# Pooled keys and values of two batches transposed by DMA through DRAM instead of by TensorE

## The chip, the cores and the metric

The kernel runs on one core of a Trainium2 chip. A core has a matrix engine (TensorE, PE in the profile; its weight loads are listed as PEld), a vector engine (VectorE, DVE), a scalar engine for activation functions (ScalarE, ACT), a general engine (GpSimd, POOL), and a sync engine (SyncE, SP) that here only issues DMA transfers. Each runs its own list of instructions in order and waits on semaphores for the others. PE writes its results to PSUM, here seen as eight banks of 128 partitions by 512 f32; everything else lives in SBUF or DRAM.

The metric is the device time of one execution in microseconds. For the kernel before it is 948.33 us, the median of 3 runs (948.24 to 948.73).

## The reference

Attention with a spatially reduced key side, then a two-layer network on every token:

```python
# q: (4, 12288, 128), kv: (4, 384, 32, 128), w_sr: (128, 128), all f32
kv_pool = kv.reshape(B, H // 4, 4, W // 4, 4, C).mean(axis=(2, 4))   # (4, 96, 8, 128)
k = v = kv_pool.reshape(B, 768, C) @ w_sr                            # keys are the values
a = softmax(q @ k.transpose(0, 2, 1) / sqrt(C))
x = (a @ v).reshape(49152, 128)
h = x @ w_in                                                         # (128, 2048)
out = (h * sigmoid(1.702 * h)) @ w_out                               # (2048, 128)
```

## The kernel before

**Tiling.** The 49152 tokens are cut into 96 groups of 512. For attention, group i has six chunks, one for each 128 of the 768 keys of its batch; for the network (called MoE in the code), group g has 16 chunks, one for each 128 of the 2048 hidden units. A chunk is *filled* by PE (one matmul of 512 columns into a PSUM bank: `fill_attn` L350, `fill_moe` L596), put through exp or GELU by ACT into a slot of the SBUF buffer `ag` (L352, L598), three chunks to an ACT instruction, and later *drained* by PE: `drain_attn` (L363) multiplies it with the values of its batch, `drain_moe` (L606) with a block of w_out. Fills use banks 0 to 2 and 3 to 5 in turn; drains accumulate in banks 6 and 7. DVE ends an attention tile by dividing by the sum of weights (L386, L389), and an MoE group by a transpose of 32x32 blocks from PSUM into one of three `o_sb` tiles (L617), which SP writes to DRAM with four DMAs (L619).

**Two rounds.** The attention of batches 0 and 1, then the MoE of their 48 groups, then the same for batches 2 and 3. Between, parts of x of 24 tiles are put away in DRAM by SP and brought back transposed (`put_away` L503, `bring_back` L509). During the first round's MoE these come one at a time: put away when group 9, 11, 13, 15, 17 begins, brought back when group 10, 12, 14, 16, 18 begins.

**Keys and values of batches 2 and 3** are made in the first round's MoE as well. Eight times two DMAs of POOL load and add kv over the window into an f32 tile (`add_kv`, from group 2 on for batch 2 and from group 24 on for batch 3; `gate` holds POOL back until DVE is so far). Then, for each half batch `a`, when group 12 or 14 (34 or 36) begins, `use_kv` lets DVE add the last two rows (`sum_kv`, L179: 96 pooled rows by 4 by 128 channels, bf16) and enters three steps in a list of extras: `transpose_pooled` (four PE transposes L184, a DVE copy into pT, L186), `make_k` (one matmul of 384 columns L192, a DVE copy into kT, L193) and `make_v` (three matmuls of 128 columns L199, a DVE copy into v, L201).

**What sets the order.** Each engine's order is written out by hand: a planner in the kernel's Python runs once when the program is built, with a clock `now` for PE, `end[p]` for the end of each ACT instruction and `dve` for DVE. Its unit is one matmul of 512 columns. It places fill after fill and, between them, drains and extras, while they fit ahead of the time at which the next fill is due (`limit`, L802). The times that it reckons with stand in a few constants; the lines that matter here are

```python
FIXED, CHUNK, SWITCH, HANDOVER, EVACUATE = 0.295, 1.978, 6.0, 1.0, 4.5      # L746
now = max(now, end[p - 2] + HANDOVER / 2)                                   # L786: the bank is free
begin = max(now + HANDOVER / 2, end[p - 1] if p else 0.0)                   # L788: ACT begins
limit = end[-1] - len(seq[n + 3][1]) - HANDOVER if n + 3 < len(seq) else 1e9  # L802
```

A sequence of work that DVE also helps with (exp and GELU of a few chunks by polynomials, `early_fill`, L415 and L409) is fixed in number and is placed by the same planner. `background_moe(g)` (L556) is called when the first fill of group g is placed, and enters the DMAs and extras of that group.

Of the kernel before, what the change touches and what calls it, by code (L numbers as in the profile page):

```python
# [10 lines left out]
BF = mybir.dt.bfloat16  # L11
# [13 lines left out]
def kernel(  # L25
    ctx, tc, q, kv, w_sr, moe_w_in, moe_w_out, out,
):
    nc = tc.nc
    B, N, C = q.shape
    _, H, W, _ = kv.shape  # L30
    r = 4
# [17 lines left out]
    q_flat = q.rearrange("b n c -> (b n) c")  # L49
    x_bf = nc.dram_tensor("x_bf", (B * N, C), BF, kind="Internal").ap()  # L50
    q_bf = nc.dram_tensor("q_bf", (B * N, C), BF, kind="Internal").ap()

    kv_r = kv.rearrange("b (ch p) (a w) c -> b a ch p (w c)", p=128, a=2)

# [43 lines left out]
    def acc_bf():  # L98
        return acc().bitcast(BF)
# [20 lines left out]
    def new_keys(b):  # L120
        kTs[b] = kvres.tile([128, J], BF, name="kT")

        vs[b] = kvres.tile([128, JC, C + 8], BF, name="v")
        nc.vector.memset(vs[b][:, :, C:C + 1], 1.0)

    def load_chunk(b, jc):
# [51 lines left out]
        pooled[b, a] = kvtmp.tile([Hp, 4, C], BF, name="pooled")  # L178
        nc.vector.tensor_tensor(pooled[b, a], t[:, 0], t[:, 1], ADD)  # L179

    def transpose_pooled(b, a):
        ps = acc_bf()[:, 0:h].rearrange("p (a b) -> p a b", a=4)
        for wp in range(4):
            nc.tensor.transpose(ps[:, wp, :], pooled[b, a][:, wp, :], ident[:Hp, :Hp])  # L184
        pTs[b, a] = kvtmp.tile([128, h], BF, name="pT")
        nc.vector.tensor_copy(pTs[b, a], ps.rearrange("p a b -> p (a b)"))  # L186

    def make_k(b, a):
        ps = acc()
        if a == 0:  # L190
            new_keys(b)
        nc.tensor.matmul(ps[:, :h], w_sr_sb, pTs[b, a], start=True, stop=True)  # L192
        nc.vector.tensor_copy(kTs[b][:, a * h:(a + 1) * h], ps[:, :h])  # L193

    def make_v(b, a):
        ps = acc()
        pT = pTs.pop((b, a))
        for k in range(K):
            nc.tensor.matmul(ps[:, k * C:(k + 1) * C], pT[:, k * 128:(k + 1) * 128], w_sr_sb,  # L199
                             start=True, stop=True)  # L200
        nc.vector.tensor_copy(vs[b][:, a * K:(a + 1) * K, 0:C], ps[:, :h].rearrange("p (k c) -> p k c", k=K))  # L201
        for jc in range(a * K, a * K + K):
            vs[b, jc] = True

# [351 lines left out]
    def background_moe(g):  # L556

        n, g = divmod(g, 4 * XS)
        m, odd = divmod(g - 9, 2)
        m += FIRST  # L560
        if n == 0 and FIRST <= m < RT // PART:
            (bring_back if odd else put_away)(n, m)
        g += n * 4 * XS
        nonlocal low
        if g == 12:
            low = EARLY * JC
            order[:] = [f for f in order if f >= low // K]
        if g in CAST_MOE:
            gate()
            cast_q(CAST_MOE[g])  # L570
        if g in (41, 42):
            load_qT(g - 28)
        if g == 43:
            background(early[0])
        for b, lo in ((2, 2), (3, 24)):
            if lo <= g < lo + 8:
                gate()
                add_kv(b, g - lo)
            if g in (lo + 10, lo + 12):
                use_kv(b, (g - lo - 10) // 2)  # L580

    def use_kv(b, a):
        nonlocal extra_at
        sum_kv(b, a)
        on_dve(3.5)
        extra_at = max(extra_at, dve + 1.5)
        extras.extend([(transpose_pooled, b, a), (make_k, b, a), (make_v, b, a)])

    extras = []

# [120 lines left out]
    def prepare(p):  # L711
# [3 lines left out]
        for i, jc in part:  # L715
# [27 lines left out]

    FIXED, CHUNK, SWITCH, HANDOVER, EVACUATE = 0.295, 1.978, 6.0, 1.0, 4.5  # L746
    COST = {pool_chunk: (1.9, 2.6), key_chunk: (0.3, 2.4), value_chunk: (0.3, 2.4),
            transpose_q: (1.05, 4.2), early_fill: (1.0, 5.5), key_and_value: (0.55, 3.5),
            transpose_pooled: (0.9, 3.6), make_k: (0.8, 3.2), make_v: (0.8, 3.7)}
    COPY = {pool_chunk: 1.5, key_chunk: 1.5, value_chunk: 1.5, key_and_value: 2.8, transpose_q: 3.2}  # L750
    SMALL = 0.26
    RECIPROCAL = 8.2
# [5 lines left out]
    def on_dve(cost):  # L758
        nonlocal dve
        dve = max(dve, now + 1.0) + cost  # L760
# [8 lines left out]
    def fill(p):  # L769
        nonlocal now  # L770
        if p >= len(seq):
            return
        kind, part = seq[p]
        prepare(p)
        if p == 4:
            turns.insert(0, 2)
        if p == narrow - 5:
            for m in (2, 5):
                turns.remove(m)
        if p == narrow:  # L780
            assert not any(m in closes for m in (2, 5))
            now = max(now, free.pop(2), free.pop(5))
        lo = K * (p % 2)
        (fill_attn if kind == "a" else fill_moe)(part, banks[:, lo:lo + len(part), :])
        if p >= 2:
            now = max(now, end[p - 2] + HANDOVER / 2)  # L786
        now += len(part)
        begin = max(now + HANDOVER / 2, end[p - 1] if p else 0.0)  # L788
        if p and kind != seq[p - 1][0]:
            begin += SWITCH  # L790
        end.append(begin + FIXED + CHUNK * len(part))
# [5 lines left out]
    for n in range(len(seq)):  # L797
        fill(n + 2)
        jobs(n + 3)
        while True:  # L800
            room = room_ahead()
            limit = end[-1] - len(seq[n + 3][1]) - HANDOVER if n + 3 < len(seq) else 1e9  # L802
            bank = free[next_acc()]
            f = None
            if extras and now >= max(extra_at, bank):
                f, *args = extras[0]
            if steps and dve <= now + 2.0:
                early_step()
            near = todo and todo[0][0] == "m" and todo[0][2] > 10
            if not f and not near and not steps and early_todo and early_fits(min(n + 2, len(seq) - 1), *early_todo[0]) and dve <= now + 2.0 and now >= bank:  # L810
                f, args = early_fill, early_todo[0]
            if f and max(now, bank) + COST[f][0] > limit + (0.0 if f is early_fill else 4.5) and room >= 4 * K:
                f = None
            if f:
                now = max(now, bank) + COST[f][0]
                f(*args)
                free[last_acc] = dve + 1.0 if f is early_fill else copied(f)
                if f in (transpose_pooled, make_k, make_v):
                    on_dve(2.5)
                extra_at = max(now + PAUSE, dve + 1.5 if f in (transpose_pooled, make_k, make_v) else 0.0)  # L820
                if f is early_fill:
                    pass
                else:
                    extras.pop(0)
                continue
            if not source:

                if todo_early and not any(early_waits(t) for t in range(todo_early[0][1], todo_early[0][1] + TS)):
                    source = todo_early
                else:  # L830
                    source = todo
            if not source:
                break
            kind, i, c = source[0]
            needs = at[("at" if kind == "a" else kind, i, c)]
            cost = K * SMALL if kind == "a" else 1.0
            halved = kind == "a" and i // TS < SPLIT
            first_of = (c == 0 or halved) and (kind == "m" or i % TS == 0)
            if source is not todo_early and (needs > n or (kind == "a" and first_of and at["at", i + TS - 1, c if halved else 1] > n)
                                             or (kind == "m" and first_of and (i, FCH - 1) in lent  # L840
                                                 and made.get((i, FCH - 1), 1e9) > now + 1.0)
                                             or (kind == "a" and (early_waits(i) or first_of and early_waits(i + TS - 1)))):
                if first_of:
                    source = None
                break
            start = now if source is todo_early else max(now, end[needs] + HANDOVER)
            if first_of:
                start = max(start, bank)
            if start + cost > limit and not (room < 2 * K + 1 or (room < 4 * K and start == now)):
                if first_of:  # L850
                    source = None
                break
            now = start + cost
            (drain_attn if kind == "a" else drain_moe)(i, c)
            source.pop(0)
            if kind == "a" and i // 4 in early:
                early_left -= 1
                if not early_left:
                    low = 0
            if (halved or c == (1 if kind == "a" else FCH - 1)) and (kind == "m" or i % TS == TS - 1):  # L860
                source = None
# [31 lines left out]
```

## Time and profile before

| | |
|---|---|
| median of 3 runs | 948.33 us (948.24 to 948.73) |
| span of the profiled execution, first to last instruction | 946.7 us |
| PE busy | 933.9 us (99%) |
| ACT busy | 933.5 us (99%) |
| DVE busy | 575.1 us (61%) |
| granted TensorE clock | 1.00 throughout |
| DMA, mean over the span | 101 GB/s |
| L184, 16 transposes of pooled keys, mean of one record | 205 ns |
| L199, 12 value matmuls, mean of one record | 219 ns |

The profile is one execution recorded by the hardware. A group in it is named by line, engine and operation, with the tile written and the tiles read (out<-in); the mean is the length of one record. Records of PE overlap, since a matmul begins before the one before it has left the array, so that the time that a matmul costs is read from the chain of waits, where each piece begins as the last one ends. SPq and POOLq are the queues of DMA issues; the time to landing of a DMA runs from its issue to its completion. "Idle before <- X" names what ended a wait.

### The profile page before, as it was taken

What the parts mean: (1) busy time and instruction counts of PE and PEld (TensorE: products, weight loads), DVE (VectorE), ACT (ScalarE), POOL (GpSimd) and SP (SyncE); (2) the same over time, 40 slices, a digit from 0 to 9 for tenths busy, and PEclk for the clock granted to TensorE, in tenths of its full rate; (3) what the DMA queues carried; (4) which work ended last, traced back from release to release, by engine and by line L of the source; (5) the groups of instructions that cost most, each with busy time, mean ns of one, the idle gap of its engine ahead of it and who ended that gap; (6) DMA issues with size and microseconds to landing.
All of it is one profiled execution on the core that took longest, in us unless ns stands there. A gap on an engine that the chain in (4) does not pass through costs nothing.

```text
span 946.7 us, 15374 instructions
## 1 busy us (share of the span) xinstructions
PE 933.9 (99%) x6200; PEld 502.5 (53%) x6314; DVE 575.1 (61%) x1091; ACT 933.5 (99%) x709; POOL 66.5 (7%) x115
## 2 busy tenths in 40 slices
PE   8999999999999999999999999999999999999998
PEld 4677776444444444444446777744444444444444
DVE  5753653011678776667765765376767766777651
ACT  6999999999999999999999999999999999999998
POOL 3101001330000232000000000000000000000000
PEclk9999999999999999999999999999999999999999
DMA  9997943999867799865335683552222222222222
GB/s 210 195 207 168 181 92 52 130 163 170 164 117 114 119 147 119 127 99 87 56 58 105 138 170 84 119 123 42 36 39 40 38 41 34 44 34 45 34 45 46
DMA packets 372856, 95.46 MB, mean 101 GB/s; under 512 B 346720, under 2 KB 370400, under 8 KB 372320
## 3 DMA queue, kind: packets, MB, share of 16 engines
q1 hardware_dynamic: 344000, 62.36, 36.9%
q0 software_dynamic: 28512, 31.99, 22.3%
q8 instruction: 49, 0.80, 0.3%
q14 instruction: 23, 0.19, 0.1%
q10 hardware_dynamic: 272, 0.13, 0.0%
HBM read 52.49 MB, written 48.76 MB: 107 GB/s over the span
## 4 chain that ended last, share of the span: by engine, by line
PE 97%; ACT 1%; DMA 1%; issue 1%; DVE 0%; POOL 0%; POOLq 0%
PE banks L606 35%; PE banks L596 34%; PE banks L363 14%; PE banks L350 12%; ACT ag L352 1%; PE banks L415 1%; DMA x<-in_kv_dram 1%; PE banks L139 0%; PE banks L409 0%; PE banks L634 0%; PE banks L236 0%; POOL x L222 0%; PE banks L161 0%; PE banks L294 0%; PE banks L192 0%
## 5 line engine op out<-in xcount | busy, mean ns | idle before, releaser
L598 ACT ACTIVATE ag<-banks 128x1536 bf16<-128x1536 f32 (+1 forms) x509 | 681.1, 1489 | 0.0
L596 PE MATMUL banks<-x,w_in_sb 128*128 128x512 bf16 x1476 | 405.8, 379 | 1.7
L606 PE MATMUL banks<-ag,w_out_sb 128*128 128x512 bf16 x1477 | 402.6, 379 | 1.7
L352 ACT ACTIVATE ag<-banks 128x1536 bf16<-128x1536 f32 (+2 forms) x192 | 245.6, 1421 | 3.5 <-PE banks L236 2.3
L606 PEld LDWEIGHTS <-w_out_sb 128*128 128x128 bf16 x1520 | 148.3, 98 | 177.2 <-issue 0.2
L596 PEld LDWEIGHTS <-w_in_sb 128*128 128x128 bf16 x1519 | 147.1, 98 | 171.3 <-issue 0.7
L617 DVE STREAM_TRANSPOSE o_sb<-banks 128x512 f32<-128x512 f32 x95 | 68.1, 717 | 171.4 <-PE banks L606 166.9
L363 PEld LDWEIGHTS <-ag 128*128 128x128 bf16 x2268 | 145.5, 98 | 44.6 <-issue 0.3
L363 PE MATMUL banks<-v,ag 128*128 128x129 bf16 x2268 | 163.0, 220 | 0.2
L350 PE MATMUL banks<-qT,kT 128*128 128x512 bf16 x498 | 145.0, 379 | 3.5 <-ACT ag L352 0.5
L442 DVE SCALAR_TENSOR_TENSOR ea<-ea,eb 128x512 f32<-128x512 f32 x132 | 90.4, 685 | 3.7 <-DVE ea L442 0.7
L386 DVE RECIPROCAL rec<-banks 128x3 f32<-128x3 f32 x124 | 22.3, 180 | 85.3 <-PE banks L363 84.9
L389 DVE TENSOR_TENSOR x<-banks,rec 128x384 bf16<-128x384 f32 x124 | 69.1, 557 | 4.3
L350 PEld LDWEIGHTS <-kT 128*128 128x128 bf16 x543 | 45.8, 98 | 25.9 <-issue 2.0
L473 DVE RECIPROCAL eb<-ea 128x256 f32<-128x256 f32 x34 | 57.6, 1724 | 0.5
L466 DVE SCALAR_TENSOR_TENSOR ea<-ea,eb 128x512 f32<-128x512 f32 x68 | 46.5, 683 | 1.9
L173 POOL DMA_DIRECT2D kvs<-in_kv_dram x32 | 40.4, 1323 | 19.3 <-DMA kvs<-in_kv_dram 17.1
L431 DVE TENSOR_SCALAR ea<-banks 128x512 f32<-128x512 f32 x33 | 22.8, 692 | 29.6 <-PE banks L415 29.2
L521 POOL MEMSET gate_tile<- 1x1 f32 x38 | 3.4, 89 | 325.8 <-DVE gate_tile L520 325.8
L453 DVE TENSOR_SCALAR qT<-banks 128x512 f32<-128x512 f32 x17 | 11.8, 692 | 20.7 <-PE banks L409 20.6
L437 DVE SCALAR_TENSOR_TENSOR eb<-eb,ea 128x512 f32<-128x512 f32 x33 | 22.8, 691 | 0.9
L444 DVE SCALAR_TENSOR_TENSOR ag<-ea,ee 128x512 bf16<-128x512 f32 x24 | 16.6, 691 | 1.2
(83 smaller groups left out, 286.3 us busy)
## 6 DMA issues: line engine op xcount, KB each, us to landing
out_dram<-o_sb SPq DMA_DIRECT2D x380, 64.0 KB, 2.0
kvs<-in_kv_dram POOLq DMA_DIRECT2D x32, 384.0 KB, 6.3
q_bf<-in_q_dram POOLq DMA_DIRECT2D x21, 512.0 KB, 6.6
x_bf<-x SPq DMA_DIRECT2D x13, 768.0 KB, 5.6
x<-in_kv_dram POOLq DMA_DIRECT2D x11, 512.0 KB, 10.4
x_bf<-x SPq DMA_DIRECT2D x6, 384.0 KB, 4.6
x<-in_q_dram POOLq DMA_DIRECT2D x5, 256.0 KB, 15.3
x<-in_kv_dram SPq DMA_DIRECT2D x1, 1024.0 KB, 5.0
```

Source lines behind the costliest of these rows:

```text
L173: nc.gpsimd.dma_start(out=kv_sums[b][:, i2], in_=kv_p[b, i, w, :, i2], **({"accum_op": ADD} if n else {}))
L350: nc.tensor.matmul(ps[:, k, :], kTs[i // GB][:, jc * 128:(jc + 1) * 128], rhs, start=True, stop=True)
L352: nc.scalar.activation(place([("a",) + c for c in chunks]), ps, AF.Exp, scale=scale)
L363: nc.tensor.matmul(av_of[u][:, k * (C + 1):(k + 1) * (C + 1)], weights(("a", i, jc))[:, o:o + T], vs[i // GB][:, jc, 0:C + 1], start=(jc = ...
L389: nc.vector.tensor_tensor(to, ps[:, :, 0:C], rec.unsqueeze(2).broadcast_to([128, TS, C]), MUL)
L442: nc.vector.scalar_tensor_tensor(a, a, COEFFS[k], b, ADD, MUL)
L466: nc.vector.scalar_tensor_tensor(a, a, COEFFS[k], b, ADD, MUL)
L473: nc.vector.reciprocal(b[:, m:m + 256], a[:, m:m + 256])
L596: nc.tensor.matmul(ps[:, k, :], w_in_sb[:, fc * 128:(fc + 1) * 128], x[:, g % (4 * XS) * G:(g % (4 * XS) + 1) * G], start=True, stop=True)
L598: nc.scalar.activation(place([("m",) + c for c in chunks]), ps, AF.Gelu_apprx_sigmoid)
L606: nc.tensor.matmul(o_of[g], w_out_sb[:, fc, :], weights(("m", g, fc)), start=(fc == 0), stop=(fc == FCH - 1))
L617: nc.vector.transpose(o_sb, o_of.pop(g))
```

## The change

The pooled half of batches 2 and 3 is no longer transposed by PE. When group 11 (14 for the second half; 33 and 36 for batch 3) begins, DVE adds the rows as before and SP writes the pooled half to a DRAM tensor (`put_pooled`). When the next group begins, SP reads it back with a transposing DMA into pT (`turn_pooled`), and when the one after that begins, `make_k` is entered in the extras. Its kT half is written to another DRAM tensor (`put_k`) at the next step, and one group later read back by three transposing DMAs into the value tile (`turn_k`): the values are the keys transposed, so `make_v` falls away. Rows of the value tile are 144 wide instead of 136.

The planner's constants change as well: ACT's fixed part of an instruction is 0.24 instead of 0.295, and HANDOVER is split into RELEASE (0.3, end of ACT to the next fill of its banks, formerly 0.5), LATENCY (0.95, end of a fill to the start of ACT, formerly 0.5) and MARGIN (1.2 in `limit`, formerly 1.0). This moves fills and drains against each other in the whole program.

```diff
@@ -49,6 +49,8 @@
+    pool_bf = nc.dram_tensor("pool_bf", (B, 2, r, Hp, C), BF, kind="Internal").ap()
+    k_bf = nc.dram_tensor("k_bf", (B, JC, C, 128), BF, kind="Internal").ap()
...
-        vs[b] = kvres.tile([128, JC, C + 8], BF, name="v")
+        vs[b] = kvres.tile([128, JC, C + 16], BF, name="v")
...
-    def transpose_pooled(b, a):
-        ps = acc_bf()[:, 0:h].rearrange("p (a b) -> p a b", a=4)
-        for wp in range(4):
-            nc.tensor.transpose(ps[:, wp, :], pooled[b, a][:, wp, :], ident[:Hp, :Hp])
-        pTs[b, a] = kvtmp.tile([128, h], BF, name="pT")
-        nc.vector.tensor_copy(pTs[b, a], ps.rearrange("p a b -> p (a b)"))
+    def put_pooled(b, a):
+        nc.sync.dma_start(out=pool_bf[b, a].rearrange("w h c -> h w c"), in_=pooled[b, a])
+
+    def turn_pooled(b, a):
+        pTs[b, a] = kvtmp.tile([128, 1, h], BF, name="pT")
+        nc.sync.dma_start_transpose(out=pTs[b, a], in_=pool_bf[b, a].rearrange("w h c -> (w h) c"))
+
+    def put_k(b, a):
+        jc = slice(a * K, a * K + K)
+        nc.sync.dma_start(out=k_bf[b, jc].rearrange("j c t -> c j t"),
+                          in_=kTs[b][:, a * h:(a + 1) * h].rearrange("c (j t) -> c j t", t=128))
+
+    def turn_k(b, a):
+        for jc in range(a * K, a * K + K):
+            nc.sync.dma_start_transpose(out=vs[b][:, jc:jc + 1, 0:C], in_=k_bf[b, jc])
 
     def make_k(b, a):
         ps = acc()
         if a == 0:
             new_keys(b)
-        nc.tensor.matmul(ps[:, :h], w_sr_sb, pTs[b, a], start=True, stop=True)
+        nc.tensor.matmul(ps[:, :h], w_sr_sb, pTs.pop((b, a))[:, 0, :], start=True, stop=True)
         nc.vector.tensor_copy(kTs[b][:, a * h:(a + 1) * h], ps[:, :h])
-
-    def make_v(b, a):
-        ps = acc()
-        pT = pTs.pop((b, a))
-        for k in range(K):
-            nc.tensor.matmul(ps[:, k * C:(k + 1) * C], pT[:, k * 128:(k + 1) * 128], w_sr_sb,
-                             start=True, stop=True)
-        nc.vector.tensor_copy(vs[b][:, a * K:(a + 1) * K, 0:C], ps[:, :h].rearrange("p (k c) -> p k c", k=K))
...
-            if g in (lo + 10, lo + 12):
-                use_kv(b, (g - lo - 10) // 2)
-
-    def use_kv(b, a):
-        nonlocal extra_at
-        sum_kv(b, a)
-        on_dve(3.5)
-        extra_at = max(extra_at, dve + 1.5)
-        extras.extend([(transpose_pooled, b, a), (make_k, b, a), (make_v, b, a)])
+            a, step = divmod(g - lo - 9, 3)
+            if 0 <= a < 2 and step == 0:
+                sum_kv(b, a)
+                on_dve(3.5)
+                put_pooled(b, a)
+            if 0 <= a < 2 and step == 1:
+                turn_pooled(b, a)
+            if 0 <= a < 2 and step == 2:
+                extras.append((make_k, b, a))
+            if 1 <= a < 3 and step == 0:
+                put_k(b, a - 1)
+            if 1 <= a < 3 and step == 1:
+                turn_k(b, a - 1)
...
-    FIXED, CHUNK, SWITCH, HANDOVER, EVACUATE = 0.295, 1.978, 6.0, 1.0, 4.5
+    FIXED, CHUNK, SWITCH, HANDOVER, EVACUATE = 0.24, 1.978, 6.0, 1.0, 4.5
+    RELEASE, LATENCY, MARGIN = 0.3, 0.95, 1.2
     COST = {pool_chunk: (1.9, 2.6), key_chunk: (0.3, 2.4), value_chunk: (0.3, 2.4),
             transpose_q: (1.05, 4.2), early_fill: (1.0, 5.5), key_and_value: (0.55, 3.5),
-            transpose_pooled: (0.9, 3.6), make_k: (0.8, 3.2), make_v: (0.8, 3.7)}
+            make_k: (0.8, 3.2)}
...
         if p >= 2:
-            now = max(now, end[p - 2] + HANDOVER / 2)
+            now = max(now, end[p - 2] + RELEASE)
         now += len(part)
-        begin = max(now + HANDOVER / 2, end[p - 1] if p else 0.0)
+        begin = max(now + LATENCY, end[p - 1] if p else 0.0)
...
-            limit = end[-1] - len(seq[n + 3][1]) - HANDOVER if n + 3 < len(seq) else 1e9
+            limit = end[-1] - len(seq[n + 3][1]) - MARGIN if n + 3 < len(seq) else 1e9
...
-                if f in (transpose_pooled, make_k, make_v):
+                if f is make_k:
                     on_dve(2.5)
-                extra_at = max(now + PAUSE, dve + 1.5 if f in (transpose_pooled, make_k, make_v) else 0.0)
+                extra_at = max(now + PAUSE, dve + 1.5 if f is make_k else 0.0)
```

## The prediction

> **What bounds the kernel now.** I read the page's busy shares first, then the same by stages, then the chain that ended last, and last the queues that the change touches. The page:
>
> ```profile
> PE 933.9 (99%) x6200; PEld 502.5 (53%) x6314; DVE 575.1 (61%) x1091; ACT 933.5 (99%) x709; POOL 66.5 (7%) x115
> ...
> PE 97%; ACT 1%; DMA 1%; issue 1%; DVE 0%; POOL 0%; POOLq 0%
> ```
>
> and of the stages the one from 75 to 945 us (its length, then busy time and count of PE, PEld, DVE, ACT, POOL, then the granted clock, DMA share and GB/s):
>
> ```profile
> 75.00:945.00 870.00, 863.08 (x5408) 455.56 (x5506) 529.99 (x951) 867.24 (x649) 51.44 (x79) 1.00 0.56 92
> ```
>
> PE and ACT are equally busy, so the busy shares do not say which of them rules. The chain does: 97% of it is PE. In the stretch from 75 to 945 us PE's records cover 863 of 870 us, and what is missing is mostly lost records: the chain has its pieces there back to back. Around the first of the steps that go:
>
> ```profile
> 228.58 0.65 PE banks L606 x3
> 229.23 0.17 PE banks L184 x4
> 229.40 0.65 PE banks L596 x3
> 230.05 0.43 PE banks L606 x2
> 230.48 0.16 PE banks L192
> 230.64 0.65 PE banks L596 x3
> 231.29 0.43 PE banks L606 x2
> 231.72 0.17 PE banks L199 x3
> ```
>
> Each piece starts where the last one ends; a full matmul (512 columns) takes 0.216 us (0.65 for three). ACT's 501 triple instructions are 1.345 us apart (673.6 us over 501 in the groups), because PE feeds them no faster. So after the start a microsecond of PE work taken away is a microsecond won, and a microsecond that PE waits is a microsecond lost. SP's queue, and PE's supply from it, is where a wait can come from:
>
> ```profile
> 212.31 6.04 SPq L619 DMA_DIRECT2D out_dram<-o_sb  x4
> 219.87 3.29 SPq L509 DMA_TRANSPOSE x<-x_bf  x1
> 223.28 2.19 SPq L619 DMA_DIRECT2D out_dram<-o_sb  x4
> 225.57 0.45 SPq L503 DMA_DIRECT2D x_bf<-x  x1
> 226.12 4.78 SPq L619 DMA_DIRECT2D out_dram<-o_sb  x4
> 231.00 3.39 SPq L509 DMA_TRANSPOSE x<-x_bf  x1
> ```
>
> SP issues in order. Here, at the pooled keys of batch 2, it is not idle: four output writes take 2.19 us to issue, but 4.78 behind a 768 KB put-away, and a bring-back holds SP 3.4 us.
>
> **The change, part by part.** *What goes.* Per half batch PE loses four transposes (0.17 us of the chain) and three value matmuls (0.17); the key matmul (0.16) stays. Four halves: 4 x 0.34 = **1.36 us off the path**, all won. DVE loses two copies per half (L186 0.36, L201 0.56 us); DVE is idle 5.97 us ahead of each output transpose of that stretch, so that wins nothing.
>
> The Trainium skill ("TensorE: Matmul & The Clock Gate", Part 4: PE-mode transpose) gives a transpose some 275 ns in a kernel. By that the 16 would cost 4.4 us and the change would win 5.1; the chain's 0.17 us for four says 42 ns each, since they overlap in the pipeline, and I go by the chain.
>
> *What is added: PE's wait for pT.* make_k now reads a pT that comes over SP: put the pooled half into DRAM, read it back transposed, one group of 512 tokens (6.7 us) apart. PE's order is fixed, and what is queued behind make_k is everything: fills, drains, and through them ACT. So its landing time counts in full. Distances are counted in the new program's order of instructions.
>
> First half of batch 2. SP's order is: put-away, pooled put, four writes of group 8, four of group 9, bring-back, then the transposing read. Group 9's writes need its last drain matmul. PE reaches make_k 33 full matmuls after that one: 34 x 0.2157 = 7.33 us from its start. The chain to pT from the same moment: 0.4 (a matmul's record is 0.38) + 0.72 (DVE's output transpose) + 2.19 (four writes) + 0.1 (gaps) + 3.39 (bring-back) = 6.8, plus the landing of a read of 384 rows. For that the rows (the last number is the median time to landing, us) are:
>
> ```profile
> out_dram<-o_sb SPq DMA_DIRECT2D x380, 64.0 KB, 2.0
> ...
> x_bf<-x SPq DMA_DIRECT2D x6, 384.0 KB, 4.6
> ...
> qT<-q_bf SPq DMA_TRANSPOSE x21, 4.2
> ...
> x<-x_bf SPq DMA_TRANSPOSE x16, 7.4
> ```
>
> Between 2.0 (64 KB, plain) and 4.2 (2048 rows, transposed) I take 2.5, because 384 rows (96 KB) stand nearer to the first; the packets of the bring-back ahead give about the same end (5.5 to its landing, then 0.5). So pT is there at 9.3, and PE waits 2.0; with the kvs loads of POOL, which crowd the queues up to 213 to 220 us, **2.3 us**. Low end: 1.95 for the writes, 2.95 for the bring-back, 2.0 for the read: 0.8 us. High end: writes at 4.78, bring-back landing at its median 7.4 and 0.5 behind it: 6.6 us.
>
> Second half of batch 2. Ahead of the read stand four writes of group 12 and two 384 KB put-aways (1.29 us to issue). PE allows 37 x 0.2157 = 7.98 us from group 12's last drain. Chain: 0.4 + 0.72 + 1.95 + 0.1 = 3.2 to the first put-away, 0.55 to the second, 4.6 to its landing, 0.5 for the read behind it: 8.8, so a wait of **0.8 us**. Low end 0, if the read passes unhindered (4.5 + 2.0); high end 2.0, if the writes take 2.70 as at 240.22 and the put-aways 0.5 more.
>
> Batch 3, both halves. No put-away or bring-back is in SP's way; PE allows 10.8 us from the last drain that SP depends on, and the chain is 0.4 + 0.72 + 1.96 + 0.1 + 2.5 = 5.7. **0**, with 5 us of slack that would even cover 4.2 and a write of 4.78.
>
> *What is moved or added elsewhere.* The 12 value reads and 4 key puts come after make_k; values are first used many groups later, so 0. SP gains about 24 issues, at most 0.5 us each, 12 us in all, in a stretch where it already waits on DVE for most of each group (L619 waited 318.7 us in total); output tiles have three buffers, so 0. sum_kv stands one group earlier on DVE, now close to the landing of the last kvs add: DVE may wait there, and the output transpose of the group is queued behind it, but 5.97 us of idleness cover that: 0, a loss of 1 us if the adds land 7 us late.
>
> *The planner's times.* In its unit (one full matmul, 0.2157 us) a triple on ACT goes from 6.229 to 6.174, 1.343 to 1.331 us; fills go a little sooner and drains later: counted in the two orders, 31 to 49 MoE chunks lie between fill and drain over most of the way instead of 23 to 39. PE has no gaps after 75 us that a better order could close, so no gain; drains stand further behind ACT, not closer, so no loss: 0. In the start PE is idle 4.2 of 75 us, and the new order could shift that by half a microsecond either way. At the end, 28 full and 64 small matmuls follow the last fill, formerly 44 small ones; the last group needs a bank nine small matmuls after the drain that frees it (9 x 0.056 = 0.5 against 0.4 + 0.72): **0.5 us** lost, between 0 and 1.1.
>
> Sum: -1.36 + 2.3 + 0.8 + 0.5 = **+2.2 us**. The profiled execution spans 946.7 us and would span 948.9; the median of the runs, 948.33, stands 1.6 above the span, which I keep: **950.6 us**.
>
> **The rivals.** *A: pT comes in time* (not slower). Both waits at their low ends: -1.36 + 0.8 + 0 + 0.3 gives 948.1, and 947.0 without any. For it speaks that the planner left a whole group between the steps; against, that SP's writes and bring-back use up that group. It decides where the first wait is below 2 us.
>
> *B: the first wait is long.* With the writes at 4.78 and the bring-back at 7.4 the sum is +5 to +8: 953 to 956. For it: the same four writes took 6.04 and 4.78 us behind 768 KB put-aways. Against: in the new order a further set of four writes stands between put-away and the ones that count, and takes up that delay. The granted clock is 1.00 in every row, and no PE gap there comes near 2 us. The Trainium skill (same page, Why this matters for your kernels) warns of PE idle for over some 3 us, after which the clock halves; a whole idle window would add, by an estimate from that page's 3.4 us window, 1.7 us. No row here shows such a drop, and my 2.3 us lies under it.
>
> *C: the hand-over times are too tight*, ACT becomes the bound and drains wait: 0.012 us by some 660 instructions is up to 8 us, 955. Against: the greater distance from fill to drain.
>
> *D: a better start* beside no waits: 946.4 or less, which needs 0.6 us of the 4.2 idle; the openings of the two orders hardly differ.
>
> **How the numbers follow.** My forecast (waits of 2 to 4.5 us in all) has 0.50, A 0.27, B 0.12, C 0.07, D 0.04. A measurement can tell about 0.2% from no change, 1.9 us: slower begins at 950.2. The forecast's span, 948.9 to 952, lies across that; 0.38 of its 0.50 above, since the waits have more room upward than down. Slower: 0.38 + 0.12 + 0.07 = 0.57; same: 0.12 + 0.27 = 0.39; faster: 0.04. The range from 948.0 to 954.0 takes in the forecast, the nearer halves of A and B and half of C. The forecast's own range is 948.9 to 952.
>
> **What would show it.** PE idle before the first make_k (L203) of batch 2 by about 2 us, under 1 us before the second, none at batch 3, each ended by the DMA pT<-pool_bf; no wait elsewhere after 75 us; ACT idle for several us at the end. I am wrong if the wait at L203 is missing or above 4 us, if the clock falls below 1.00 behind it, or if drains wait for ACT.

## The result and the profile after

The changed kernel takes 957.16 us, the median of 4 runs (957.05 to 957.31), against 948.52 us for the kernel before, measured beside it (948.24 to 948.73): a ratio of 1.0092, with a 95% interval of 1.0078 to 1.0107. It is 8.6 us slower, and the spans of the profiled executions, 955.3 and 946.7 us, differ by the same 8.6. The prediction was 950.6, with a range up to 954.0: the sign was the likeliest one, and the size was wrong by 6.6 us.

The page's totals and its chain by engine, of the kernel after:

```profile
PE 945.2 (99%) x6286; PEld 501.0 (52%) x6286; DVE 569.8 (60%) x1083; ACT 933.2 (98%) x709; POOL 66.4 (7%) x115
ACT 71%; PE 25%; DMA 2%; SPq 1%; issue 1%; DVE 0%; POOL 0%; DVEq 0%; POOLq 0%
```

ACT is busy for the same time as before (933.5 us), and yet the chain of waits, which had been 97% PE, is now 71% ACT. PE is still called 99% busy. A record of a full matmul is 0.38 us long while matmuls follow each other every 0.2157 us, so a delay of some hundredths of a microsecond between two of them leaves no gap between their records, and the busy share can't show it.

What PE waited for at the moved step, and what ACT waited for at the end (list of waits: total us, count, longest):

```profile
ACT o_sb L649 <- PE banks L641: 8.5, 1, 8.5
...
PEld L203 <- DMA pT<-pool_bf: 3.2, 2, 1.9
...
PE banks L203 <- DMA pT<-pool_bf: 2.2, 2, 1.5
```

The two waits at `make_k` (L203) are the ones that the prediction named: two, both in batch 2, both ended by the transposing read. Measured from the start of one matmul to the start of the next, less the 0.2157 us that it takes anyway, they cost 1.6 and 0.95 us. That is 2.6 us of the 10.0 that have to be found (8.6, and the 1.36 us of removed work). The 8.5 us of ACT are at the very end, where it waits for PE's last drains. The timeline of PE there, of the kernel before first (start us, us, what):

```profile
940.35 0.59 PE L596 MATMUL banks<-x,w_in_sb 128*128 128x512 bf16 x2
940.78 2.62 PE L634 MATMUL banks<-w_out_sb,ag 128*128 128x128 bf16 x44
```

and of the kernel after:

```profile
941.32 0.59 PE L603 MATMUL banks<-x,w_in_sb 128*128 128x512 bf16 x2
941.75 6.21 PE L613 MATMUL banks<-ag,w_out_sb 128*128 128x512 bf16 x28
947.79 0.67 PE L641 MATMUL banks<-w_out_sb,ag 128*128 128x128 bf16 x9
948.76 3.23 PE L641 MATMUL banks<-w_out_sb,ag 128*128 128x128 bf16 x55 [0.30 <-DVE o_sb L624]
```

This is nearly the whole difference. The last fill begins only 1.0 us later than before (941.32 against 940.35), so ACT, which has its last work from it, ends 1.0 us later. But 28 full drain matmuls and 20 more small ones are left for the time behind it: 28 x 0.2157 + 20 x 0.0555 = 7.15 us. Before the last 55 small ones PE waits 0.47 us for a bank (0.30 in the record, the rest by spacing of starts). 1.0 + 7.15 + 0.47 = 8.6.

So the question is why drains that had room between the fills before are now left over. The groups of ACT hold the clue, the kernel before first, then after (last columns: busy us, mean ns of one record, idle ahead):

```profile
L598 ACT ACTIVATE ag<-banks 128x1536 bf16<-128x1536 f32 x501 | 673.6, 1496 | 0.0
```

```profile
L605 ACT ACTIVATE ag<-banks 128x1536 bf16<-128x1536 f32 x501 | 673.8, 1614 | 1.6 <-PE banks L603 1.4
```

The busy time over the count is 1.345 us in both. The mean *record*, 1.496 us, is longer than that: records overlap, each beginning before the last one has ended. It has grown to 1.614, which points to more work lying ready for ACT, not less: of the kernels below, one in which PE is relieved has the longest records and one in which ACT is fed late the shortest. The chain says the same: in this stretch in mid-run it is ACT alone, one instruction behind the other, where in the kernel before (shown second) it is PE alone:

```profile
699.28 7.79 ACT ag L605 x6
707.07 0.04 issue
707.12 5.59 ACT ag L605 x4
```

```profile
703.11 0.65 PE banks L606 x3
703.76 0.65 PE banks L596 x3
704.40 0.86 PE banks L606 x4
```

Theory 1: ACT was full in the kernel before already, at 1.343 us for a triple. That is the median distance between the ends of successive records in every run, and in the kernel before 483 of 499 such distances lie between 1.340 and 1.346 us (in the kernel below in which ACT is fed late, 353 of 499). The old FIXED says just that: (0.295 + 3 x 1.978) x 0.2157 = 1.344 us. The new one says 0.24, or 1.332 us. With it the planner believes ACT to be 0.012 us faster per instruction than it is; over its 662 triple instructions the planner's ACT runs ahead by up to 7.9 us. Fills are placed too early and wait for their banks, a little each time, drains that would have fitted into that time aren't placed there, and they are left at the end.

The starts of PE's records show these small waits, counted after 75 us and over fills that start 0.01 to 0.08 us later than PE's pace (0.2157 us behind a full matmul, 0.057 behind an attention drain): 193 fills of the kernel after, 0.035 us on average, 6.7 us in all. With the 2.6 at `make_k` and the 0.5 at the end this is 9.8 of the 10.0. In the kernel before there are 5 such fills, 0.2 us in all. It is ACT that they wait for: of the late fills that follow a drain, all but a few begin 0.050 to 0.052 us after an ACT record ends, while half of those of the kernel before begin 0.27 us or more after one.

The rivals are: that the hand-over times (RELEASE, LATENCY, MARGIN) do it; that the way through DRAM does it, by the waits and by what they upset; or that PE, not ACT, sets the pace in the kernel before, as the prediction said.

### The profile page after: what moved, and what is told of

Same layout as the page of the kernel before. It is cut to its first block, busy times and chain, and to the rows that moved or that the text cites. A ratio compares the mean times of both kernels' runs of the same rounds, so it can differ in the third digit from the quotient of the medians.

```text
span 955.3 us, 15468 instructions
## 1 busy us (share of the span) xinstructions
PE 945.2 (99%) x6286; PEld 501.0 (52%) x6286; DVE 569.8 (60%) x1083; ACT 933.2 (98%) x709; POOL 66.4 (7%) x115
## 4 chain that ended last, share of the span: by engine, by line
ACT 71%; PE 25%; DMA 2%; SPq 1%; issue 1%; DVE 0%; POOL 0%; DVEq 0%; POOLq 0%
ACT ag L605 58%; ACT ag L355 13%; PE banks L366 7%; PE banks L353 6%; PE banks L603 6%; PE banks L613 5%; DMA x<-in_kv_dram 1%; DMA pT<-pool_bf 1%; PE banks L141 0%; SPq L512 0%; PE banks L641 0%; SPq L626 0%; DVE o_sb L624 0%; DMA out_dram<-o_sb 0%; ACT L605 0%
## 5 line engine op out<-in xcount | busy, mean ns | idle before, releaser
L603 PE MATMUL banks<-x,w_in_sb 128*128 128x512 bf16 x1519 | 410.4, 378 | 0.1
L353 PE MATMUL banks<-qT,kT 128*128 128x512 bf16 x543 | 148.4, 378 | 1.4 <-ACT ag L355 0.5
```

The costliest lines, as they stand in the source:

```text
L353: nc.tensor.matmul(ps[:, k, :], kTs[i // GB][:, jc * 128:(jc + 1) * 128], rhs, start=True, stop=True)
L603: nc.tensor.matmul(ps[:, k, :], w_in_sb[:, fc * 128:(fc + 1) * 128], x[:, g % (4 * XS) * G:(g % (4 * XS) + 1) * G], start=True, stop=True)
```

## The experiments

**Is ACT or PE the bound before?** The kernel before, without every second MoE drain matmul: 665 matmuls fewer, 143 us of PE's time.

```diff
-        nc.tensor.matmul(o_of[g], w_out_sb[:, fc, :], weights(("m", g, fc)),
-                         start=(fc == 0), stop=(fc == FCH - 1))
+        if fc % 2 == 0 or fc == FCH - 1:
+            nc.tensor.matmul(o_of[g], w_out_sb[:, fc, :], weights(("m", g, fc)),
+                             start=(fc == 0), stop=(fc == FCH - 1))
```

> The kernel before without every second drain matmul of the MoE, 665 full matmuls fewer, 143 us of PE's time (a part of the network's second product is left out, so the output is not the reference's); everything else, ACT's instructions included, as before. If ACT's own pace is 1.3435 us (theory 1), PE's relief wins almost nothing: 944 to 948, and ACT's groups keep 1.34 us each. If PE alone bounds the kernel and ACT could go at 1.331 or faster (the prediction's reading): 939 or less.

Measured: 948.37 us in one run, span 946.6, beside 948.46 for the kernel before. 15% of PE's work taken away (143 of 934 us) wins nothing. The page's chain, the group and the wait that goes with it:

```profile
ACT 95%; PE 3%; DMA 1%; issue 1%; POOL 0%; DVE 0%; POOLq 0%
```

```profile
L598 ACT ACTIVATE ag<-banks 128x1536 bf16<-128x1536 f32 x501 | 673.2, 1752 | 0.0
```

```profile
PE banks L596 <- ACT ag L598: 44.7, 141, 0.5
```

PE now waits for ACT at its fills, in 141 places, and the pace of ACT is still 673.2/501 = 1.344 us: it is ACT's own. In the kernel before both engines are full at once, and its chain, 97% PE, is no evidence that ACT is fed late: between two engines that are both 99% busy it followed one.

**Which constant?** Three kernels with the old way by TensorE. All of the new times in the kernel before:

```diff
-    FIXED, CHUNK, SWITCH, HANDOVER, EVACUATE = 0.295, 1.978, 6.0, 1.0, 4.5
+    FIXED, CHUNK, SWITCH, HANDOVER, EVACUATE = 0.24, 1.978, 6.0, 1.0, 4.5
+    RELEASE, LATENCY, MARGIN = 0.3, 0.95, 1.2
...
-            now = max(now, end[p - 2] + HANDOVER / 2)
+            now = max(now, end[p - 2] + RELEASE)
-        begin = max(now + HANDOVER / 2, end[p - 1] if p else 0.0)
+        begin = max(now + LATENCY, end[p - 1] if p else 0.0)
...
-            limit = end[-1] - len(seq[n + 3][1]) - HANDOVER if n + 3 < len(seq) else 1e9
+            limit = end[-1] - len(seq[n + 3][1]) - MARGIN if n + 3 < len(seq) else 1e9
```

> The kernel before with the planner's new times alone (ACT's fixed part 0.24, RELEASE 0.3, LATENCY 0.95, MARGIN 1.2); transposes stay on PE. Theory 1 (ACT's own pace is 1.3435 us per triple, as the ends of its records stand apart; the planner that reckons with 1.331 runs 0.012 us per triple ahead of it, some 8 us over 660, so fills come before their banks are free, PE waits there and its drains are left over for the end): 955 to 957.5, ACT's last record at the same time as before, 28 or so full matmuls behind it. Theory 2 (the way through DRAM and its waits make the loss, the planner's times nothing): 948 to 949.

Measured: 957.17 us (956.80 to 957.33), ratio 1.0091 (1.0075 to 1.0108). The whole loss is there without a single transfer moved. 35 full and 64 small matmuls follow its last fill in the program, and its ACT group is as in the kernel after:

```profile
L598 ACT ACTIVATE ag<-banks 128x1536 bf16<-128x1536 f32 x501 | 673.2, 1625 | 0.0
```

Only the first of those lines, FIXED 0.24:

> The kernel before with ACT's fixed part 0.24 instead of 0.295 and nothing else. Theory 1: 955 to 957.5, the whole of the loss less the waits for pT. Theory 3 (the earlier fill after ACT's end, RELEASE 0.3 for 0.5, is what makes PE wait, 0.04 us each time): 948 to 949.5.

Measured: 956.99 us (956.80 to 957.25), ratio 1.0091 (1.0076 to 1.0106), and the same 35 full and 64 small matmuls behind the last fill. ACT waits for them (list of waits):

```profile
ACT o_sb L642 <- PE banks L634: 10.0, 1, 10.0
```

Only the others, RELEASE, LATENCY and MARGIN, with FIXED left at 0.295:

> The kernel before with RELEASE 0.3, LATENCY 0.95 and MARGIN 1.2, but ACT's fixed part left at 0.295. Theory 1 (the fixed part alone makes the loss): 948 to 949. Theory 3 (the earlier fill after ACT's end matters too): 950 to 957.

Measured: 948.68 us (948.50 to 948.96, 10 runs), ratio 1.0001 (0.9992 to 1.0011). The hand-over times proper do nothing that can be measured, and only 9 fills are late by the count above, 0.3 us in all; the rival that they are to blame falls.

**Is it the pace?** If FIXED must match ACT's pace, a value between must lose less, and a value above 0.295 must lose as well, in the opposite way: fills come too late, and ACT idles. FIXED 0.2675 in the kernel before:

```diff
-    FIXED, CHUNK, SWITCH, HANDOVER, EVACUATE = 0.295, 1.978, 6.0, 1.0, 4.5
+    FIXED, CHUNK, SWITCH, HANDOVER, EVACUATE = 0.2675, 1.978, 6.0, 1.0, 4.5
```

> The kernel before with ACT's fixed part at 0.2675, half way to 0.24. Theory 1 (the planner's clock for ACT runs ahead by the error times the number of ACT's instructions, 0.0059 us by some 660): 4 us lost, 952 to 953.5, with about half as many full matmuls left over behind the last fill. If the loss comes from a threshold (a bank missed or not): near 948.5 or near 957.

Measured: 954.09 us (953.91 to 954.40), ratio 1.0059 (1.0042 to 1.0075): 5.6 us slower, where the theory's 0.006 us by 662 gave 4. The timeline of PE at its end:

```profile
939.38 0.59 PE L596 MATMUL banks<-x,w_in_sb 128*128 128x512 bf16 x2
939.81 4.05 PE L606 MATMUL banks<-ag,w_out_sb 128*128 128x512 bf16 x18
943.69 0.67 PE L634 MATMUL banks<-w_out_sb,ag 128*128 128x128 bf16 x9
944.66 3.23 PE L634 MATMUL banks<-w_out_sb,ag 128*128 128x128 bf16 x55 [0.30 <-DVE o_sb L617]
```

18 full matmuls and 20 more small ones than before are left: 3.9 + 1.1 us, and the wait of 0.47 for the bank, together 5.5. (The last fill begins 1.0 us earlier than in the kernel before, and the span ends 1.0 us later behind PE's last matmul; the two cancel.) The late fills are 134, with 4.0 us in all, against 6.9 us in 198 at FIXED 0.24: that part follows the error as the theory has it. The loss as a whole isn't proportional, because the 1.6 us of small matmuls and bank wait come whole at both values. Without them it is 3.9 against 7.5 us (35 full) at 0.24, about half.

FIXED 0.35, as far above 0.295 as 0.24 lies below:

```diff
-    FIXED, CHUNK, SWITCH, HANDOVER, EVACUATE = 0.295, 1.978, 6.0, 1.0, 4.5
+    FIXED, CHUNK, SWITCH, HANDOVER, EVACUATE = 0.35, 1.978, 6.0, 1.0, 4.5
```

> The kernel before with ACT's fixed part at 0.35, as far above 0.295 as 0.24 is below. Theory 1 (ACT's true pace is 6.23 units, 0.295): the planner now thinks ACT slower than it is and fills come late, so ACT waits about 0.012 us per triple: 954 to 957, with ACT waiting on PE and no full matmuls left over at the end. If 0.295 were only a safe margin above a faster ACT, a greater margin would cost the same again as the last one, and going down from 0.295 would have won: not seen above; then 948 to 950 here.

Measured: 955.57 us (955.48 to 955.74), ratio 1.0074 (1.0059 to 1.0089). Its group of ACT:

```profile
L598 ACT ACTIVATE ag<-banks 128x1536 bf16<-128x1536 f32 x501 | 679.0, 1457 | 0.1
```

Now ACT itself is slowed: 679.0/501 = 1.355 us, the planner's pace ((0.35 + 5.934) x 0.2157 = 1.355), with the shortest records of all, 1.457. The 5.4 us more here and 1.6 us more in the 161 attention triples (218.7 against 217.1) are 7.0 of the 7.2 that it loses. No full matmul is left at the end, and of the small waits at fills, counted as above, there are only 9. So of the four values tried 0.295 is the best, and the two sides of it are told apart by the profile: too small leaves drains over, too large leaves ACT short.

**What does the way through DRAM cost by itself?** The kernel after with the old times:

```diff
-    FIXED, CHUNK, SWITCH, HANDOVER, EVACUATE = 0.24, 1.978, 6.0, 1.0, 4.5
-    RELEASE, LATENCY, MARGIN = 0.3, 0.95, 1.2
+    FIXED, CHUNK, SWITCH, HANDOVER, EVACUATE = 0.295, 1.978, 6.0, 1.0, 4.5
+    RELEASE, LATENCY, MARGIN = 0.5, 0.5, 1.0
```

> The changed kernel with the planner's old times (ACT's fixed part 0.295, RELEASE 0.5, LATENCY 0.5, MARGIN 1.0, which is the old reckoning); transposes through DRAM. Theory 1: 948 to 950.5, namely the waits for pT of 2 to 3 us less the 1.36 us of PE work saved, or less if ACT still has work in stock. Theory 2: 956 to 958, no better than the change.

Measured: 952.66 us, but in two kinds of runs: 952.76, 952.58 and 952.75, and one of 950.27 (ratio 1.0039, 1.0024 to 1.0054). The profiled one is of the long kind. PE's timeline at the first `make_k`:

```profile
238.09 0.34 PE L203 MATMUL banks<-pT,w_sr_sb 128*128 128x384 bf16 x1 [2.97 <-DMA pT<-pool_bf]
238.26 0.81 PE L613 MATMUL banks<-ag,w_out_sb 128*128 128x512 bf16 x2
238.86 1.49 PE L603 MATMUL banks<-x,w_in_sb 128*128 128x512 bf16 x3
```

and the windows around it (us, PE busy, PEld, DVE, ACT, POOL, then the granted clock):

```profile
235.00:238.50 3.50, 0.53 (x4) 0.23 (x4) 0.04 (x1) 1.75 (x2) 0.00 (x0) 1.00 0.85 180
238.50:242.00 3.50, 3.50 (x10) 1.29 (x9) 0.52 (x1) 1.45 (x1) 0.00 (x0) 0.51 0.79 180
242.00:245.00 3.00, 2.95 (x15) 1.35 (x14) 1.28 (x2) 2.26 (x2) 0.00 (x0) 1.00 0.45 113
```

After 2.97 us of idleness the clock was granted at half from 238.5 to 241.9 us, for 3.41 us; three fills take 1.49 us instead of 0.81. That is the drop that the prediction's rival B was afraid of. The same kernel again, for ten runs:

> The changed kernel with the planner's old times once more, beside the one in which only SP's order differs. Theory 1: again PE's wait of 3 us before the first make_k; where it covers a whole window of idleness the clock falls for 3.4 us and the time is 952.5, where it does not, 950.3, so single runs of this kernel lie at one or the other.

Measured: 950.09 us, ratio 1.0020 (1.0010 to 1.0029); nine of ten runs lie between 949.74 and 950.84, and one at 952.33. Its mean clock was 0.998, as in the three long runs above; the ten short ones have 0.999 or 1.000. In the profiled one PE waits 2.0 us and the clock stays 1.00:

```profile
PE banks L203 <- DMA pT<-pool_bf: 2.0, 1, 2.0
```

So with the right pace, the way through DRAM alone costs 1.7 us (950.09 against 948.40), the wait of 2.0 us less a little, and about 2.4 us more in 4 of its 14 timed executions, those with the lower mean clock. In the one of the four that was profiled the wait is 3 us and the clock falls; that the other three did the same is inferred from their clock.

The rule for this is in the Trainium skill ("TensorE: Matmul & The Clock Gate", Part 1: The HAM clock gate): a gate that watches PE in free-running windows of some 3.4 us and lets through half of the clock pulses after an idle one. The half rate and the 3.41 us agree with these rows; the 2.97 us of measured idleness are less than one such window. In the kernel after itself no wait reached 2 us and the clock was 1.00 throughout.

**Can the wait be had away?** It comes from the order of SP's issues, in the kernel after:

```profile
224.12 5.87 SPq L626 DMA_DIRECT2D out_dram<-o_sb  x8
230.03 3.22 SPq L512 DMA_TRANSPOSE x<-x_bf  x1
233.30 1.25 SPq L188 DMA_TRANSPOSE pT<-pool_bf  x1
```

The bring-back of 3072 rows (L512) keeps SP for 3.22 us just ahead of the transposing read of 384 rows, which PE is waiting for. So the read is issued first:

```diff
     def background_moe(g):
+        for b, lo in ((2, 2), (3, 24)):
+            a, step = divmod(g - lo - 9, 3)
+            if 0 <= a < 2 and step == 1:
+                turn_pooled(b, a)
         n, g = divmod(g, 4 * XS)
...
-            if 0 <= a < 2 and step == 1:
-                turn_pooled(b, a)
```

With all the new times:

> The changed kernel with all its new times, and the transposing read issued ahead of the bring-back and put-aways. Theory 1: PE's two waits for pT (1.6 and 0.95 us in the changed kernel) vanish; PE is late at the end by the matmuls left over, so their time comes off in full: 954.3 to 955.5, unless ACT's pace alone sets how many are left over, then 957.

Measured: 954.99 us (954.87 to 955.23), ratio 1.0068 (1.0053 to 1.0083), and no wait at `make_k`. The two waits were worth 2.2 us of the 957.16. With FIXED 0.295 and the other new times:

> The changed kernel with ACT's fixed part back at 0.295 (the other new times kept), and the transposing read of the pooled half issued ahead of the bring-back and the put-aways that begin with the same group. Theory 1: PE's waits for pT vanish or stay under 0.5 us, as SP is free 3.3 us sooner; with ACT full, the 1.36 us of PE work saved win little: 947.3 to 948.6. If SP's order is not what makes pT late, the first wait stays at 2 us or more and the time is 950 or more.

Measured: 948.12 us (947.97 to 948.39, 10 runs), ratio 0.9996 (0.9986 to 1.0005). With all the old times:

> The changed kernel with all the planner's old times, and the transposing read issued ahead of the bring-back and the put-aways. Against the kernel with the old times and SP's order as changed (952.66, where PE waited about 3 us before the first make_k and the granted clock then fell to 0.5 for 3.4 us), only SP's order differs. Theory 1: no wait at make_k, clock 1.00 throughout, 947.5 to 948.7. If the loss there had another cause than SP's order: 950 or more.

Measured: 948.08 us (947.88 to 948.43, 10 runs), ratio 0.9996 (0.9987 to 1.0005) against 948.40. The queue of SP and the time to landing in this kernel (the last number is the median in us):

```profile
228.87 2.10 SPq L628 DMA_DIRECT2D out_dram<-o_sb  x4
231.07 1.11 SPq L188 DMA_TRANSPOSE pT<-pool_bf  x1
232.28 2.99 SPq L512 DMA_TRANSPOSE x<-x_bf  x1
```

```profile
pT<-pool_bf SPq DMA_TRANSPOSE x4, 2.6
```

In the kernel after that median had been 5.1, but the order of issues isn't all of it. Its four reads landed 2.6, 4.3, 6.3 and 5.8 us after their issue: the first, right behind the bring-back, as fast as here, and the last two, in batch 3, slowly with no put-away or bring-back ahead. What the swap saves at the first `make_k` is the issue of the bring-back, 3.22 us, and not a slow landing; at the second it is both (4.3 us to landing there, 2.6 here).

The steps between after and before are now all measured, each beside a kernel before at 948.52: 957.16 with everything, 954.99 with the read first, 948.12 with FIXED 0.295 as well, 948.52 before. So of the 8.6 us, 2.2 are the waits, 6.9 are FIXED, and -0.4 is what remains of the change, a difference whose interval includes none. That last step is the work taken off PE, 1.36 us by the prediction, and with FIXED 0.295 it won about nothing, as ACT is full there. In another order the shares differ: FIXED 0.24 alone costs 8.5 us; with all the new times, taking the work off PE (without the waits) then wins 2.2 (957.17 to 954.99), of which 1.5 are 7 full matmuls fewer at the end; and the waits cost these 2.2 again.

No kernel here is shown to be faster than the one before. Waiting to start `make_k` by a further group was not tried, nor giving DVE more of ACT's chunks.

## Why the prediction was wrong, point by point

**The step that failed** is the paragraph on the planner's times: "PE has no gaps after 75 us that a better order could close, so no gain; drains stand further behind ACT, not closer, so no loss: 0." The runs show +8.5 us for FIXED alone in the kernel before (956.99 against 948.46) and +6.9 with the read first. The argument was on the wrong event. It asked whether a *drain* would come before its GELU was done; the greater distance in the order is indeed a protection against that, and the list of waits of the kernel after names no MoE drain that waits for it. What comes too early is the *fill*, which needs the bank that ACT hasn't emptied yet, and the same greater distance is the stock of drains that is left over at the end. The prediction had even counted it: 31 to 49 chunks instead of 23 to 39, and "28 full and 64 small matmuls follow the last fill, formerly 44 small ones". It had also named "ACT idle for several us at the end" among the signs that it was right. It priced of this only the 0.5 us for the bank (0.47 measured) and not the 7.15 us of matmuls, because it held the sum of PE's work to be what sets the end, so that a matmul at the end was one less in the middle. That is right only as long as PE is never held up in the middle.

**Behind it stands a false reading**, "ACT's 501 triple instructions are 1.345 us apart ..., because PE feeds them no faster". The number was right and the reason wrong: 1.344 us is ACT's pace with half of the drains taken away as well. Neither the length of the records nor the idle time ahead of the group tells it: with FIXED 0.35, where ACT is fed late, the mean record of 1457 ns is longer than its spacing of 1355 too, and idle ahead is 0.1. Two things in the profile before could have told. The ends of its records were 1.343 us apart nearly without exception (483 of 499 within 1.340 to 1.346), as of an engine at its own pace. And the old FIXED gave 1.344, so that 1.332 claims a different pace for ACT, which these ends contradict. The starts mislead here: in the kernel before, the median distance between starts is 1.331 us and that between ends 1.343 us, over the same 501 records. For some instructions on end the starts are 1.331 us apart while the records grow by about 12 ns each and the ends stay 1.343 apart. The ends, or busy time over count, are the pace.

The Trainium skill ("ScalarE: Activation LUTs", What ACT_TABLE_LOAD costs) gives 186 ns and 0.833 ns for each element of a partition, less an overlap of 93 ns, for an ACTIVATE with immediate operands. By an estimate from that, 1536 elements take 1.373 us back to back. This case's traces have 1.343, 2% less, so the measurement decides; an estimate that is off by 0.030 us can't tell 1.344 from 1.332.

**Rival C** was therefore the right one as to its engine and size ("ACT becomes the bound ...: 0.012 us by some 660 instructions is up to 8 us, 955"), and was given 0.07 on the strength of the same false argument on drains; its waits are at fills. The range of the prediction held half of it only.

**The work removed, -1.36 us "all won"**: wrong for a kernel in which ACT is full. With no waits and the old times the gain is 0.3 us, with an interval from a gain of 1.2 to a loss of 0.5. Only with the new times, where PE's leftover drains set the end, was it won: 28 full matmuls there instead of 35.

**The waits at `make_k`**: right in place, number, cause and, nearly, in size. Forecast 2.3 and 0.8 us, and 0 for batch 3; measured 1.6 and 0.95, and 0. The terms of the first: the bring-back 3.39, measured 3.22; the landing of the read 2.5, measured 2.6. The two waits together cost 2.2 us of the time, forecast 3.1. The 0 for batch 3 was in part luck: the landings there were forecast at 2.5 us and took 6.3 and 5.8, so that pT came only 1.1 and 0.4 us before PE reached `make_k`, where the prediction had 5 us of slack. "No wait elsewhere after 75 us" was wrong, at the fills. **SP's further issues, `sum_kv`**: nothing was seen of them in the time, as forecast: with the read first and FIXED 0.295 nothing is left to explain. **Rival B** was possible: the clock did fall, though in the kernel with the old times and not in this one.

What stays open: the kernel after and the one with the new times alone take the same time (957.16 and 957.17). In the profiled executions the last fill of the first begins 1.9 us later (941.32 against 939.43), for its waits, and 7 full matmuls fewer follow it (1.5 us). The 0.4 us between, and what the ends behind PE's last matmuls differ by (0.6 us the other way), weren't traced.

## What to carry to other kernels

A planner's price for an instruction must be the pace at which records of that instruction *end* in a full queue (busy time over count), and an error of about 1% in it, in either direction, cost about 1% of the kernel here: too fast leaves the other engine's work over at the end, too slow starves the engine itself. Where two engines are both 99% busy the chain of waits may name either; taking work off one of them, as an experiment, settles which holds the time. On a queue that issues in order, a small transfer that a bound engine waits for belongs ahead of the long ones: one such swap took 2.2 us off.

## What was unexpected of the hardware

ACT's records lengthen with the work that lies ready, without its pace changing: mean records of 1496, 1614 and 1752 ns went with 1.345, 1.345 and 1.344 us of busy time for each (1457 ns with 1.355 us where ACT was fed late). PE's granted clock fell to half after 2.97 us of idleness, for 3.41 us, and the same kernel, with a wait of 2.0 us in another execution, kept 1.00; its times come in two kinds, 2.4 us apart, told apart by the mean clock. And the landing of a transposing read of 384 rows from DRAM varied without an evident order: in the kernel after it took 2.6 us right behind the bring-back of 3072 rows, 4.3 us behind two put-aways, and 6.3 and 5.8 us in batch 3, where neither stands ahead.
